# Routing's modality bias computed in the opening, its loads on another queue, and head 0's value rest released earlier

## The chip, the cores and the metric

The program runs on one core of a Trainium2 chip, in one launch. The metric is the device time of an execution in microseconds; of the kernel before there are three timed runs and one execution under the hardware profiler. The core's engines are TensorE (PE in the profile, PEld its weight loads), VectorE (DVE), ScalarE (ACT), GpSimd (POOL) and SyncE (SP), which here issues most DMAs. Each takes its own instructions in order.

## The reference, cut to what matters

Attention with rotary embedding over 2 batches x 8 heads of 576 tokens, then a mixture of 8 experts with one expert for each token, then a dense layer pair with a gate:

```
attn_out = softmax(rot(q) @ rot(k).T / 8) @ v          # 16 heads, 576 x 64 each
x = attn_out as (1152 tokens, 512)
logits = x @ w_gate + modality_bias[modality_id]       # 8 experts
e_idx = argmax(logits); gate_w = softmax(logits)[e_idx]
x = gate_w * (relu(x @ w1[e_idx]) @ w2[e_idx])
h = x @ w_in; g = h * tanh(softplus(h)); out = g @ w_out
```

The change touches how modality_bias[modality_id] comes to be: a table of 2 x 8 numbers, picked for each token by its modality of 0 or 1.

## The kernel before

**Arithmetic.** Products that need float32's accuracy are made of two halves: a rounded value ("hi") and the rest ("lo" = value - hi). So q, k, v, the exponentials and all weights are split by ScalarE, VectorE and GpSimd before TensorE takes them.

**Stages.** Attention's sixteen heads come first, up to about 165 us. The experts' tiles follow, then the gated layer pair. Routing of batch 0 is worked in between the later heads' work, as VectorE has room.

**Preparation of a head** n (heads 2 to 15): SyncE loads q and k as the tile xs (line 880) and v as vraw (line 884). GpSimd multiplies xs by the rotary tables (line 924), adds the halves (928), rounds (934) and takes the rest (943); both go into a tile ab, of which there is one. SyncE then copies ab into the "stack" that TensorE reads: the hi half of q (line 951, p_top), the lo half of q (959), and k hi and lo into sk twice (960, 961), all in p_stack. For v, GpSimd rounds (934, v_hi) and takes the rest (968, v_lo) into vhl. Two raw tiles vraw serve in turn: head 2's load needs head 0's tile, which its rounding and its rest read. Heads 0 and 1 are special: head 0 is rotated by p_first on VectorE, ScalarE and GpSimd without a stack; head 1 by VectorE and ScalarE, and its stack is copied as the others'.

**What follows in a head.** TensorE's scores (979) go to two PSUM tiles; VectorE takes the maximum (1003), ScalarE the exponential (1014); TensorE transposes (1027); ScalarE and VectorE split the transposed tile (1047, 1053); TensorE multiplies by v (1068), ScalarE evacuates (1077), TensorE transposes back with the gate's product appended (1098), VectorE normalizes into X (1108).

**What sets the order.** The class Plan does, when the program is built. Each step is an op with an engine, an assumed duration, a due key and the steps it depends on; the planner lets each engine take the step that could start first, or with the smaller key, and writes the instructions out in that order. Buffers and copies are steps or resources of it too (("vraw", n) is given back by the step vlo of the head two before). So an op's key, duration or dependency changes the order of all engines. What stands on an engine's list waits for semaphores at run time; a wait holds all that stands behind it there.

**The bias.** setup_ids issued two small loads from ScalarE's queue: the modalities (mod, 10 KB) and the two rows of the table spread to 128 partitions (mbias). setup_bias then worked on GpSimd: a cast, a comparison with 0 and one with 1, and for each batch two products and a sum, 40 elements wide. They stand in the plan as the ops ids (key 30) and bias (key 60, deps ids).

Of the kernel before, what the change touches and what calls it, by code (L numbers as in the profile page):

```python
# [10 lines left out]
F32 = mybir.dt.float32  # L11
# [3 lines left out]
ALU = mybir.AluOpType  # L15
# [3 lines left out]
B, H, S, D = 2, 8, 576, 64  # L19
HALF_D = D // 2  # L20
DM = H * D
NE = 8
# [190 lines left out]
def moe_kernel(ctx: ExitStack, tc: tile.TileContext, aps, out):  # L213
    nc = tc.nc
# [9 lines left out]
    kp = xctx.enter_context(tc.tile_pool(name="kp", bufs=1, side="right"))  # L224
# [16 lines left out]
    mod = kp.tile([128, B, 5, 2], I32, name="mod")  # L241
# [4 lines left out]
    def setup_consts():  # L246
        nc.vector.memset(zero, 0.0)
        nc.gpsimd.memset(ones, 1.0)
        nc.gpsimd.affine_select(
            out=upper, in_=ones, pattern=[[1, 128]], compare_op=ALU.is_gt, fill=0.0,  # L250
            base=0, channel_multiplier=-1,
        )
        nc.gpsimd.iota(
            iota8, pattern=[[0, 5], [1, NE]], base=-NE, channel_multiplier=0,
            allow_small_or_imprecise_dtypes=True,
        )
        nc.gpsimd.memset(iota8[64:128, 2, :], 1000.0)
        nc.gpsimd.iota(
            iotat, pattern=[[1, NS[1]]], base=0, channel_multiplier=0,
            allow_small_or_imprecise_dtypes=True,  # L260
        )
        for b in range(B):
            nc.gpsimd.memset(X[b][:, :, XC + 2:], 0.0)
            for j, (q0, _) in enumerate(QT):
                nc.gpsimd.iota(
                    X[b][:, j, XC:XC + 1], pattern=[[0, 1]], base=b * S + q0,
                    channel_multiplier=1, allow_small_or_imprecise_dtypes=True,
                )
    def setup_ids():
        nc.scalar.dma_start(  # L270
            out=mod.rearrange("p b j w -> p (b j w)"), in_=aps["modality"].bitcast(I32)
        )
        nc.scalar.dma_start(
            out=mbias.rearrange("p m e -> p (m e)"),
            in_=aps["modality_bias"].rearrange("(o m) e -> o (m e)", o=1).to_broadcast(
                [128, 2 * NE]
            ),
        )
# [8 lines left out]
        )  # L287

    def setup_bias():
        m = kp.tile([128, B, 5], F32, name="mf")  # L290
        sel = kp.tile([128, 2, B, 5], F32, name="msel")
        tmp = kp.tile([128, B, 5, NE], F32, name="mtmp")
        nc.gpsimd.tensor_copy(m, mod[:, :, :, 0])
        for v in range(2):
            nc.gpsimd.tensor_scalar(
                out=sel[:, v], in0=m, scalar1=float(v), scalar2=None, op0=ALU.is_equal
            )
        for b in range(B):
            sh = [128, 5, NE]
            for v, o in ((0, lbias), (1, tmp)):  # L300
                nc.gpsimd.tensor_tensor(
                    out=o[:, b], in0=sel[:, v, b, :, None].to_broadcast(sh),
                    in1=mbias[:, None, v].to_broadcast(sh), op=ALU.mult,
                )
            nc.gpsimd.tensor_tensor(out=lbias[:, b], in0=lbias[:, b], in1=tmp[:, b], op=ALU.add)


    regs = {}
# [518 lines left out]
    def attention(actx, hook):  # L827
# [26 lines left out]
        def setup_mov():  # L854
            for z in range(2):
                r = slice(z * 64, z * 64 + 64)
                nc.sync.dma_start(
                    out=mov[r, :, D:XW], in_=aps["w_gate"].rearrange("(h p) e -> p h e", p=D)
                )
                nc.vector.tensor_copy(  # L860
                    mov[r, :, 0:64],
                    ident[r, None, z * 64:z * 64 + 64].to_broadcast([64, H, 64]),
                )
# [252 lines left out]
        v_load(1)  # L1116
        p_load(2)
        setup_mov()
        setup_consts()
        p_first()  # L1120
        for n in range(2):
# [14 lines left out]
        def op(name, eng, dur, key, fn, *a, deps=(), line=None, **kw):  # L1136
            go = (lambda: fn(*a)) if isinstance(eng, str) else lambda: fn(*a, plan.eng)
            plan.op((name,) + a, eng, dur, key, go, deps=deps, line=line, **kw)

        for n in range(B * H):  # L1140
            z = 10.0 * n
            if n > 2:
                op("load", "sp", 0.45, z + K["ld"], p_load, n, take=[("xs", n)], tail=3.6, line="l")
            if n > 1:
                op("vload", "sp", 0.45, z + K["ld"], v_load, n, take=[("vraw", n)], tail=3.0, line="v",
                   deps=[("stack", 1)] * (n == 3))
            pr = K["prep"]
            if n > 1:
                op("mul", ("pool", "dve"), (2.67, 1.27), z + pr[0], p_mul, n,
                   deps=[("load", n)] + [("plo", 1)] * (n == 2))  # L1150
                op("add", ("pool", "dve"), (1.38, 0.67), z + pr[0], p_add, n, deps=[("mul", n)])
                op("phi", ("pool", "act"), (0.74, 0.573), z + pr[1], p_hi, n, deps=[("add", n)],
                   take=[("ab", n)])
                op("plo", ("pool", "dve"), (1.36, 0.669), z + pr[2], p_lo, n, deps=[("phi", n)],
                   give=[("xs", n)])
            if n == 1:
                plan.op(("add", 1), "dve", 0.67, -55.0, lambda: p_add(1, "dve"),
                        deps=[("mul", 1)])
                plan.op(("phi", 1), "act", 0.573, -50.0, lambda: p_hi(1, "act"),
                        deps=[("add", 1)], take=[("ab", 1)])  # L1160
                plan.op(("top", 1), "sp", 0.6, -50.0, lambda: p_top(1), deps=[("phi", 1)],
                        take=[("qs", 1)])
                plan.op(("plo", 1), "dve", 0.669, -50.0, lambda: p_lo(1, "dve"),
                        deps=[("phi", 1)], give=[("xs", 1)])
            if n:
                op("stack", "sp", 2.5, z + pr[3], p_stack, n, deps=[("plo", n)] + [("top", 1)] * (n == 1),
                   take=[("qs", n)] * (n > 1), give=[("ab", n)], tail=2.3)
            if n > 1:
                op("vhi", ("pool", "act"), (0.52, 0.36), z + pr[4], v_hi, n, deps=[("vload", n)],
                   take=[("vhl", n)])  # L1170
                op("vlo", ("pool", "dve"), (0.82, 0.402), z + pr[5], v_lo, n, deps=[("vhi", n)],
                   give=[("vraw", n)])
            else:
                op("vlo", "pool", 0.82, z + pr[5], v_lo, n, deps=[("vhi", n), ("plo", 1)],
                   give=[("vraw", n)])
        tiles, groups, was, e_was = 0, 0, (), ()
        for q in range(4 * (B * H) // 2):
# [53 lines left out]
            groups += len(u.groups)  # L1231
        for i in range(14):
            op("zero", "sp", 0.5, 20.0 + 5.0 * i, setup_dma, i, deps=[("stack", 3 + i // 3)])
        op("ids", "act", 0.1, 30.0, setup_ids)
        op("bias", "pool", 2.5, 60.0, setup_bias, deps=[("ids",)])
        hook(plan, bank, ltile)
        plan.run()

# [556 lines left out]
```

## Time and profile before

| | us |
|---|---|
| median of three runs (lowest, highest) | 485.17 (484.85, 485.33) |
| the profiled execution | 485.32 |
| its span, first to last instruction | 483.6 |
| TensorE busy | 464.2 (96%) |
| VectorE busy | 390.4 (81%) |
| GpSimd busy | 361.9 (75%) |
| ScalarE busy | 331.2 (68%) |

Busy shares are means over the whole span. TensorE's busy time is modelled and holds short gaps between matmuls, so what a stage is bound by is read from who waits for whom there. The chain of work that ended last is TensorE's for most of the second half of the program, with a part of VectorE's around 304 to 356 us; it can be followed back to 220 us, before which TensorE is busy nearly without a break to about 24 us.

### The profile page before, as it was taken

The numbers are of one execution on the slowest core, as the hardware profiler recorded it, in microseconds if no ns is written. First come the engines' busy times: TensorE is split into PE (matmuls) and PEld (weight loads), VectorE is DVE, ScalarE is ACT, GpSimd is POOL, SyncE is SP. The second block draws the span as 40 slices with busy tenths as digits, with TensorE's granted clock in tenths as the row PEclk, the third lists the DMA queues.
The fourth block names the chain that finished last, engine by engine and source line by source line (L and its number), as shares of the span: only waits on it lengthen the run. The fifth ranks groups of instructions, "written<-read, shape, count | busy, mean of one in ns | idle before, by whom it ended". The sixth has DMA issues, their size and how long they took to land.

```text
span 483.6 us, 8783 instructions
## 1 busy us (share of the span) xinstructions
PE 464.2 (96%) x2996; PEld 427.7 (88%) x2996; DVE 390.4 (81%) x616; ACT 331.2 (68%) x753; POOL 361.9 (75%) x363
## 2 busy tenths in 40 slices
PE   2799999999999999999999999999999999999995
PEld 1699999999998999999999998989889887888894
DVE  6599899798898765655888689999999859777773
ACT  3588888777878665475554587666675788776763
POOL 3799999999981588768767277786786749987654
PEclk9999999999999999999999999999999999999999
DMA  7689985877765399977974400202000001100002
GB/s 225 168 200 243 224 239 149 193 205 178 182 162 171 136 386 385 330 300 262 378 279 186 174 2 1 79 10 87 1 0 1 1 1 43 45 22 1 1 0 89
DMA packets 24131, 69.41 MB, mean 144 GB/s; under 512 B 5522, under 2 KB 9810, under 8 KB 22034
## 3 DMA queue, kind: packets, MB, share of 16 engines
q1 hardware_dynamic: 21794, 63.16, 42.1%
q0 software_dynamic: 1456, 5.03, 2.7%
q10 hardware_dynamic: 832, 0.61, 0.5%
q8 instruction: 25, 0.41, 0.3%
q14 instruction: 24, 0.20, 0.1%
HBM read 49.08 MB, written 6.44 MB: 115 GB/s over the span
## 4 chain that ended last, share of the span: by engine, by line
PE 41%; DVE 8%; issue 3%; POOL 1%; ACT 1%; POOLq 0%; DVEq 0%; ACTq 0%
PE h L1588 15%; PE o L1649 15%; PE mm L712 11%; DVE ta L1614 6%; DVE wc L1418 1%; DVE ta L1615 1%; POOL out_dram L1659 0%; DVE wc L1408 0%; PE mm L675 0%; DVE wc L1413 0%; POOLq L1791 0%; POOL g L1632 0%; DVE idi L1735 0%; ACT ot L1655 0%; DVE yl L1526 0%
## 5 line engine op out<-in xcount | busy, mean ns | idle before, releaser
L1614 DVE RECIPROCAL ta<-ta 128x320 f32<-128x320 f32 (+1 forms) x64 | 124.6, 1947 | 21.5 <-ACT ta L1607 20.0
L1562 POOL TENSOR_TENSOR w2l<-wc,w2h 128x512 fp32r<-128x512 f32 x64 | 89.3, 1417 | 15.3 <-ACT w2h L1561 15.3
L1649 PE MATMUL o<-w2h,g 128*128 128x512 f32 x288 | 97.8, 395 | 0.1
L1632 POOL TENSOR_TENSOR g<-ta,g 128x320 fp32r<-128x320 f32 (+1 forms) x63 | 52.7, 841 | 27.9 <-ACT g L1626 21.3
L979 PE MATMUL sc<-sk,sq 128*128 128x288 f32 (+1 forms) x320 | 59.4, 315 | 11.5 <-ACT sk L908 7.7
L1588 PE MATMUL h<-yl,w2h 128*128 128x320 f32 (+2 forms) x204 | 67.0, 328 | 0.1
L1588 PE MATMUL h<-yh,w2h 128*128 128x320 f32 (+2 forms) x204 | 66.9, 328 | 0.0
L1588 PE MATMUL h<-yh,w2l 128*128 128x320 f32 (+2 forms) x204 | 66.9, 328 | 0.0
L1649 PEld LDWEIGHTS o<-w2h,g 128*128 128x128 f32 x288 | 53.9, 188 | 12.2 <-POOL g L1632 1.0
L1047 ACT ACTIVATE ph<-pt 128x512 fp32r<-128x512 f32 (+2 forms) x112 | 54.8, 509 | 13.4 <-PE pt L1027 12.4
L1014 ACT ACTIVATE pexp<-sc,nm 128x576 f32<-128x576 f32 x72 | 53.3, 740 | 15.5 <-DVE nm L1003 11.7
L1003 DVE TENSOR_REDUCE nm<-sc 128x1 f32<-128x576 f32 x72 | 53.7, 753 | 10.8 <-PE sc L979 6.7
L979 PEld LDWEIGHTS sc<-sk,sq 128*128 128x128 f32 (+1 forms) x320 | 46.6, 190 | 14.3 <-ACT sk L908 8.1
L1649 PE MATMUL o<-w2l,g 128*128 128x512 f32 x144 | 56.8, 394 | 0.0
L1027 PE MATMUL pt<-ident,pexp 128*128 128x128 f32 (+1 forms) x360 | 55.0, 277 | 0.7 <-DVE tbl L523 0.6
L1068 PE MATMUL av<-ph,vhl 128*128 128x256 f32 (+1 forms) x160 | 50.7, 333 | 0.0
L1053 DVE TENSOR_TENSOR pl<-pt,ph 128x512 fp32r<-128x512 f32 (+1 forms) x80 | 48.8, 628 | 2.1 <-ACT ph L1047 1.8
L1027 PEld LDWEIGHTS pt<-ident,pexp 128*128 128x128 f32 (+1 forms) x360 | 42.1, 138 | 3.6 <-issue 0.7
L1626 ACT ACTIVATE g<-ta 128x320 fp32r<-128x320 f32 (+1 forms) x64 | 27.9, 436 | 22.9 <-DVE ta L1615 22.5
L1603 ACT ACTIVATE ta<-h 128x320 f32<-128x320 f32 (+1 forms) x64 | 25.5, 399 | 25.0 <-PE h L1588 23.5
L1588 PEld LDWEIGHTS h<-yl,w2h 128*128 128x128 f32 x204 | 38.3, 188 | 4.1 <-DVE yl L1526 0.4
L1588 PEld LDWEIGHTS h<-yh,w2h 128*128 128x128 f32 x204 | 38.3, 188 | 3.9 <-DVE ta L1615 0.2
(448 smaller groups left out, 1203.7 us busy)
## 6 DMA issues: line engine op xcount, KB each, us to landing
wr<-in_wio_dram SPq DMA_DIRECT2D x16, 1024.0 KB, 6.1
wc<-in_w_dram SPq DMA_DIRECT2D x26, 512.0 KB, 5.7
xs<-in_qk_dram SPq DMA_DIRECT2D x15, 576.0 KB, 5.2
sk<-ab SPq DMA_DIRECT2D x30, 288.0 KB, 3.3
sq<-ab SPq DMA_DIRECT2D x30, 144.0 KB, 2.4
vraw<-in_v_dram SPq DMA_DIRECT2D x16, 160.0 KB, 3.9
scratch<-zero SPq DMA_DIRECT2D x12, 108.8 KB, 4.8
xrow(0, 0)_2295<-scratch SPq DMA_DIRECT2D x2, 290.0 KB, 3.1
```

Of the source, the lines that this page charges most:

```text
L712: nc.tensor.matmul(ps[:, :T], lhsT=w, rhs=m, start=(n == 0), stop=(n == 3 * len(pairs) - 1))
L979: nc.tensor.matmul(t[:m, hf, :NC2], lhsT=sq[:, c:c + m], rhs=sk[:, z, hf * NC2:(hf + 1) * NC2], start=(z == 0), stop=(z == 1),)
L1003: nc.vector.tensor_reduce(out=nm[n, j], in_=sc[n, j][:, :, :NC2], axis=AX.XY, op=ALU.max, negate=True)
L1014: nc.scalar.activation(out=pe, in_=sc.pop((n, j))[:, :, :NC2], func=AF.Exp, bias=nm.pop((n, j)), accum_out=st[n, hf][:, i:i + 1],)
L1027: nc.tensor.transpose(out=t[:kn, o:o + 128], in_=pexp[n, j][:, k0:k0 + kn], identity=ident)
L1047: nc.scalar.activation(out=block(ph, n, hf, kts, slice(0, kn)), in_=psum(n, hf, kts, kn), func=AF.Copy)
L1068: nc.tensor.matmul(av[n, hf][:, :u.nq], lhsT=vhl[n][:, kt].rearrange("p a d -> p (a d)"), rhs=src[:, kt, u.at:u.at + u.nq], start=(kt == 0 ...
L1562: nc.gpsimd.tensor_tensor(out=lo[:, cs], in0=w[:, cs], in1=hi[:, cs].bitcast(F32), op=ALU.subtract)
L1588: nc.tensor.matmul(ps[:, :w], lhsT=wt[:, c], rhs=m[y][:, c], start=(n == 0), stop=(n == 11))
L1614: nc.vector.reciprocal(out=ta, in_=ta)
L1632: eng.tensor_tensor(out=gt[q][1][:, o:o + w], in0=tas.pop((q, i))[:, :w], in1=gt[q][0][:, o:o + w].bitcast(F32), op=ALU.subtract,)
L1649: nc.tensor.matmul(acc[g, t], lhsT=a[:, s], rhs=b, start=(f == 0 and z == 0), stop=(f == FC2 - 1 and z == 2),)
```

## The change

setup_ids moves from ScalarE's queue to SyncE's, behind the loads of the gate weights, and is called before the plan. setup_bias makes both products over both batches at once: six operations, the products and the sum 80 wide. Its op has the key -20, the duration 1.4 and no dependency. Head 0's value rest (vlo, 0) depends on head 1's addition instead of head 1's rest.

```diff
     def setup_ids():
-        nc.scalar.dma_start(
+        nc.sync.dma_start(
             out=mod.rearrange("p b j w -> p (b j w)"), in_=aps["modality"].bitcast(I32)
         )
-        nc.scalar.dma_start(
+        nc.sync.dma_start(
             out=mbias.rearrange("p m e -> p (m e)"),
...
     def setup_bias():
-        m = kp.tile([128, B, 5], F32, name="mf")
-        sel = kp.tile([128, 2, B, 5], F32, name="msel")
-        tmp = kp.tile([128, B, 5, NE], F32, name="mtmp")
-        nc.gpsimd.tensor_copy(m, mod[:, :, :, 0])
+        m = kp.tile([128, B * 5], F32, name="mf")
+        sel = kp.tile([128, 2, B * 5], F32, name="msel")
+        tmp = kp.tile([128, 2, B * 5, NE], F32, name="mtmp")
+        nc.gpsimd.tensor_copy(m, mod.rearrange("p b j w -> p (b j) w")[:, :, 0])
         for v in range(2):
             nc.gpsimd.tensor_scalar(
                 out=sel[:, v], in0=m, scalar1=float(v), scalar2=None, op0=ALU.is_equal
             )
-        for b in range(B):
-            sh = [128, 5, NE]
-            for v, o in ((0, lbias), (1, tmp)):
-                nc.gpsimd.tensor_tensor(
-                    out=o[:, b], in0=sel[:, v, b, :, None].to_broadcast(sh),
-                    in1=mbias[:, None, v].to_broadcast(sh), op=ALU.mult,
-                )
-            nc.gpsimd.tensor_tensor(out=lbias[:, b], in0=lbias[:, b], in1=tmp[:, b], op=ALU.add)
+        for v in range(2):
+            nc.gpsimd.tensor_tensor(
+                out=tmp[:, v], in0=sel[:, v, :, None].to_broadcast([128, B * 5, NE]),
+                in1=mbias[:, v, None].to_broadcast([128, B * 5, NE]), op=ALU.mult,
+            )
+        nc.gpsimd.tensor_tensor(
+            out=lbias.rearrange("p b j e -> p (b j) e"), in0=tmp[:, 0], in1=tmp[:, 1], op=ALU.add
+        )
...
         setup_mov()
+        setup_ids()
         setup_consts()
...
-                op("vlo", "pool", 0.82, z + pr[5], v_lo, n, deps=[("vhi", n), ("plo", 1)],
+                op("vlo", "pool", 0.82, z + pr[5], v_lo, n, deps=[("vhi", n), ("plo" if n else "add", 1)],
                    give=[("vraw", n)])
...
-        op("ids", "act", 0.1, 30.0, setup_ids)
-        op("bias", "pool", 2.5, 60.0, setup_bias, deps=[("ids",)])
+        op("bias", "pool", 1.4, -20, setup_bias, deps=[])
```

What this does to the order shows at three places. On SyncE's queue in the opening (mov are the gate weights, sq and sk the stack of head 1 as copied from ab, vraw a head's values, xs a head's q and k) there stood, before and now:

```order
L857 DMA mov<-in_w_gate_dram 64x8x8 x2
L951 DMA sq_201<-ab_192 64x576
L959 DMA sq_201<-ab_192 64x576
L960 DMA sk_202<-ab_192 64x1152
L961 DMA sk_202<-ab_192 64x1152
L884 DMA vraw_242<-in_v_dram 128x320
L880 DMA xs_250<-in_qk_dram 128x1152
```

```order
L857 DMA mov<-in_w_gate_dram 64x8x8 x2
L270 DMA mod<-in_modality_dram 128x20
L273 DMA mbias<-in_modality_bias_dram 128x16
L951 DMA sq_213<-ab_203 64x576
L884 DMA vraw_225<-in_v_dram 128x320
L959 DMA sq_213<-ab_203 64x576
L960 DMA sk_214<-ab_203 64x1152
L961 DMA sk_214<-ab_203 64x1152
L880 DMA xs_262<-in_qk_dram 128x1152
```

The two small loads come behind the gate weights, and head 2's value load has moved from behind head 1's stack to between its first copy and the other three.

On GpSimd in the opening, from the rest of head 0's q (sq) on (stt are sums of exponentials, rs their reciprocals to be, vhl the split values):

```order
L898 TENSOR_TENSOR sq_154<-xs_119,sq_154 64x320
L1086 TENSOR_SCALAR rs_1_211<-stt 128x2
L968 TENSOR_TENSOR vhl_172<-vraw_126,vhl_172 128x5x64
L924 TENSOR_TENSOR xs_130<-xs_130,tabs 128x1152
L928 TENSOR_TENSOR xs_130<-xs_130 128x576
L934 TENSOR_SCALAR ab_265<-xs_130 128x576
L943 TENSOR_TENSOR ab_265<-xs_130,ab_265 128x576
```

```order
L898 TENSOR_TENSOR sq_156<-xs_119,sq_156 64x320
L293 CAST mf<-mod 128x10
L295 TENSOR_SCALAR msel<-mf 128x10 x2
L299 TENSOR_TENSOR mtmp<-msel,mbias 128x80 x2
L303 TENSOR_TENSOR lbias<-mtmp 128x80
L968 TENSOR_TENSOR vhl_174<-vraw_126,vhl_174 128x5x64
L1086 TENSOR_SCALAR rs_1_223<-stt 128x2
L924 TENSOR_TENSOR xs_130<-xs_130,tabs 128x1152
```

The bias stands between the rest of q and head 0's value rest, and the value rest now comes ahead of the sums.

On TensorE, the first place where its order differs is between the scores of head 10 (counts are the routing's token counts, pt transposed exponentials):

```order
L979 MATMUL sc_111<-sk_1408,sq_1407 128x288 x4
L979 MATMUL sc_110<-sk_1408,sq_1407 128x288 x4
L1027 MATMUL pt_1_2_1628<-ident,pexp_3_1562 128x128
L1027 MATMUL pt_1_2_1628<-ident,pexp_4_1575 128x128
L1027 MATMUL pt_1_2_1628<-ident,pexp_3_1562 128x128
L1027 MATMUL pt_1_2_1628<-ident,pexp_4_1575 128x128
L1098 MATMUL xo_0_1633<-mov,avt_113 128x72 x3
```

```order
L979 MATMUL sc_111<-sk_1367,sq_1366 128x288 x4
L370 MATMUL counts<-oh_1582,ones 128x40
L371 MATMUL counts<-oh_1582,upper 128x40
L979 MATMUL sc_110<-sk_1367,sq_1366 128x288 x4
L1098 MATMUL xo_0_1651<-mov,avt_113 128x72 x3
```

The routing's counts come earlier, the transposes there later; from here on to the end of attention the order is another one, with the same work in it.

## Rows read from the trace of the kernel before

**Rows 1.** Busy time by stretch: start:end, length, engines' busy us (instructions), clock, DMA.

```profile
20.00:80.00 60.00, 58.81 (x473) 57.34 (x472) 51.75 (x104) 49.10 (x122) 56.17 (x67) 1.00 0.88 224
```

**Rows 2.** TensorE's waits, 7 to 190 us: total us, times, longest.

```profile
PE sc L979 <- DMA sk<-ab: 0.6, 1, 0.6
PE pt L1027 <- DVE tbl L523: 0.6, 1, 0.6
```

**Rows 3.** Line 961, the last copy of a stack: from issue to landing.

```profile
DMA to landing us min/median/max: 4.1/4.2/4.3
```

**Rows 4.** Timeline, SyncE's queue and TensorE around head 9: start, us, what, idle before.

```profile
85.33 0.60 SPq L961 DMA_DIRECT2D sk<-ab  x1
...
89.58 1.28 PE L979 MATMUL sc<-sk,sq 128*128 128x288 f32 x8 [0.61 <-DMA sk<-ab]
```

**Rows 5.** Timeline of TensorE in the opening.

```profile
14.17 1.06 PE L1027 MATMUL pt<-ident,pexp 128*128 128x128 f32 x4
...
19.76 0.67 PE L1098 MATMUL xo<-mov,avt 128*128 128x72 f32 x4 [0.47 <-ACT avt L1077]
20.22 1.82 PE L979 MATMUL sc<-sk,sq 128*128 128x288 f32 x12
23.23 0.79 PE L979 MATMUL sc<-sk,sq 128*128 128x288 f32 x4 [1.19 <-ACT pexp L1014]
23.86 1.15 PE L1027 MATMUL pt<-ident,pexp 128*128 128x128 f32 x9
```

**Rows 6.** Timeline of SyncE's queue in the opening.

```profile
4.59 1.32 SPq L857 DMA_DIRECT2D mov<-in_w_gate_dram  x2
...
14.33 0.50 SPq L959 DMA_DIRECT2D sq<-ab  x1
14.88 0.60 SPq L960 DMA_DIRECT2D sk<-ab  x1
15.54 0.59 SPq L961 DMA_DIRECT2D sk<-ab  x1
16.23 0.72 SPq L884 DMA_DIRECT2D vraw<-in_v_dram  x1
```

**Rows 7.** Timeline of GpSimd, the bias where it stood.

```profile
73.15 0.19 POOL L293 CAST mf<-mod 128x10 f32<-128x10 int32 x1
...
73.85 0.27 POOL L301 TENSOR_TENSOR lbias<-msel,mbias 128x40 f32<-128x40 f32 x1
74.06 0.27 POOL L301 TENSOR_TENSOR mtmp<-msel,mbias 128x40 f32<-128x40 f32 x1
74.41 0.27 POOL L305 TENSOR_TENSOR lbias<-lbias,mtmp 128x40 f32<-128x40 f32 x1
...
75.42 0.46 POOL L934 TENSOR_SCALAR vhl<-vraw 128x320 fp32r<-128x320 f32 x1
```

**Rows 8.** Timeline of GpSimd in the opening.

```profile
11.11 1.00 POOL L898 TENSOR_TENSOR sq<-xs,sq 64x320 fp32r<-64x320 f32 x1 [7.47 <-ACT sq L917]
14.43 0.22 POOL L1086 TENSOR_SCALAR rs<-stt 128x2 f32<-128x2 f32 x1 [2.31 <-ACT pexp L1014]
14.73 0.86 POOL L968 TENSOR_TENSOR vhl<-vraw,vhl 128x320 fp32r<-128x320 f32 x1
```

**Rows 9.** Line 968 (ns min/median/max); line 1562, 380 to 450 us; timeline at 308 us.

```profile
L968 POOL TENSOR_TENSOR vhl<-vraw,vhl x16: 858/874/884, 14.7 to 139.5; 128x320 fp32r<-128x320 f32 x16
...
L1562 POOL TENSOR_TENSOR w2l<-wc,w2h 128x512 fp32r<-128x512 f32 x24 | 30.6, 1295 | 2.8 <-ACT w2h L1561 2.8
...
308.08 3.53 POOL L1562 TENSOR_TENSOR w2l<-wc,w2h 128x512 fp32r<-128x512 f32 x2
...
308.50 1.97 DVE L1418 SCALAR_TENSOR_TENSOR wc<-wr,wc 128x1024 int32<-128x1024 int32 x1
```

**Rows 10.** Timeline of VectorE in the opening.

```profile
10.03 1.36 DVE L924 TENSOR_TENSOR xs<-xs,tabs 128x1152 f32<-128x1152 f32 x1
...
11.98 0.75 DVE L928 TENSOR_TENSOR xs<-xs 128x576 f32<-128x576 f32 x1
...
13.54 0.76 DVE L943 TENSOR_TENSOR ab<-xs,ab 128x576 fp32r<-128x576 f32 x1
```

## What was predicted

> **What bounds the kernel now.** I read the stretches first, then TensorE's waits, then the opening instruction by instruction. From 20 to 80 us TensorE is busy 58.81 of 60 us and GpSimd 56.17 of 60 [rows 1]: in attention both run almost without a break, and a reader could take either for the bound. TensorE's waits decide it [rows 2]: from 7 to 190 us it waits for the stacked copy of a head (the DMAs into sk) once only, for 0.6 us. All other heads are there when TensorE comes for them, so behind the opening TensorE sets the pace, and GpSimd keeps up closely without holding it. The one wait is head 9's: its last key copy is issued at 85.33 us and lands 4.2 us later, 89.53, and TensorE starts its scores at 89.58 after 0.61 us of idleness [rows 3, 4].
>
> The opening is different: there TensorE waits for a chain. It takes up head 1's first scores at 20.22 us, right behind the four products that end attention's first unit, and then stands still again until 23.23 for an exponential [rows 5]. Head 1's copies are issued at 14.33 (low half of q), 14.88 and 15.54 us (k twice) [rows 6], so the last one lands at 15.54 + 4.2 = 19.74. It is no more than 20.22 - 19.74 = 0.5 us early. **Whatever delays these three issues by more than 0.5 us moves everything behind it.** From 23.86 us TensorE has no long wait to swallow a shift, and the tail of the program hangs on TensorE's order, so such a shift goes to the end whole.
>
> **Part 1: the bias leaves the middle.** The old eight steps of setup_bias stand on GpSimd from 73.15 to 75.42 us, 2.27 us [rows 7], between two heads' preparation. Taking them out brings head 9's copies some 2.3 us forward, and so TensorE's wait of 0.6 us at 89.58 goes [rows 2, 4]. More can't come directly: no other wait on a stack is left. I book -0.6.
>
> **Part 2: the bias in the opening.** GpSimd's next work after the rest of head 0's q, which ends at 11.11 + 1.00 = 12.11, is at 14.43 us [rows 8]: a gap of 2.3 us. How long are the new operations? The cast and two compares are as before: 0.70 us from the cast's start to the first product's (73.15 to 73.85) [rows 7]. A 40-wide product follows the next after 0.21 us and takes 0.27; a 320-wide value rest takes 0.874 [rows 7, 9], which is (0.874 - 0.27) / 280 = 2.16 ns an element, so 80 wide is 0.09 us longer: 0.30 from one product to the next. The sum of two products starts 0.35 us after the second of them (74.06 to 74.41), 0.44 with the width, and leaves after 0.30. Together 0.70 + 0.30 + 0.44 + 0.30 = 1.74 us. Alone, they fit the gap: 12.11 + 1.74 = 13.85, and head 0's value rest, which before ran at 14.73, would run from 13.85 to 14.72. The two small loads are issued behind the gate weights (4.59 + 1.32 = 5.91 us) [rows 6], six us ahead of their use; I cost them at nothing. If they came late they would push the bias by as much.
>
> They are not alone. VectorE adds head 1's halves from 11.98 to 12.73 and takes its rest from 13.54 to 14.30 [rows 10], both with two inputs from SBUF, and the bias reads SBUF. What that does is seen later in this trace [rows 9]: a GpSimd rest w2l takes 1.295 us where VectorE decodes nothing, but a pair of them takes 3.53 us at 308.08, where VectorE starts a 1024-wide step with two SBUF inputs at 308.50. That step itself lasts 1.97 us. Read in turn: the first w2l to 309.38, then VectorE to 310.47 (1.09 us), then the second w2l. They alternate, one blocks the other. In the opening, too, q's rest of 320 elements takes 1.00 us beside the end of VectorE's long product [rows 8, 10], where a value rest of as many takes 0.874.
>
> [...]
>
> So the cast waits for 12.73 instead of 12.11 (0.62 us), and the second product waits while VectorE's rest, which comes at 13.54 during the first product (13.43 to 13.73), runs to some 14.45 (0.72 us). That is 1.34 us together: head 0's value rest runs from 15.19 to 16.06.
>
> **Part 3: what stands behind the value rest.** Head 0's rest no longer waits for head 1's rest in the plan but for its addition, so the planner thinks the buffer of raw values free earlier and puts head 2's value load between head 1's first q copy and its other three copies on SyncE's queue. That load must wait for head 0's value rest, which reads the buffer, and a waiting instruction holds all behind it. Before, the load came last, at 16.23 us, and held nothing [rows 6]. Now the low half of q is issued not at 14.33 but after the value rest (16.06 + 0.03), the load's own 0.72 us and 0.05 between issues: 16.86, 2.5 us later. The last key copy goes out at 18.07 and lands at 22.27, and head 1's scores start at 22.32 instead of 20.22: +2.1 us. Recorded ends reach 0.06 us past the next start (73.85 + 0.27 against 74.06) [rows 7], and two such seams lie in the sum, so I take **+2.0**. Bounds: without the exclusion the value rest ends at 14.72, the q copy goes at 15.52, 1.19 later, and the scores start at 20.98: +0.8. The load is of 160 KB and might slow the copies behind it; if it took its own issue time once more, +0.7 on top.
>
> GpSimd itself comes later with its next steps by as much, since its conversion of head 2 needs the buffer that head 1's copies read; head 2's and head 3's stacks then land about 2.1 to 2.5 us later, and TensorE comes 2.0 us later, so I expect at most some tenths of waiting there.
>
> **Part 4: the new order from about 100 us on.** The planner spreads the small change: TensorE's order is the same up to head 10's scores, then the routing counts come two groups of work earlier, and VectorE's table of tiles comes earlier too. Work is equal. What an order can shed or add is waits like the one on the table (0.6 us) [rows 2]; I take 0, with 0.9 us either way.
>
> **Sum.** The profiled execution took 485.32 us with a span of 483.6; the median of three is 485.17, 0.15 below. 485.32 + 2.0 - 0.6 = 486.7, less 0.15: **486.6 us**, slower by 0.3%.
>
> **Rivals.**
> *No exclusion in the opening.* The bias instructions are short and may slip between VectorE's reads; then 485.17 + 0.8 - 0.6 = 485.4, no change. For it: the rows that show blocking are of long operations; against it: q's rest of 1.00 us in the same stretch. Chance 0.25.
> *GpSimd is the bound after all.* Then its 2.27 us come off, and the new order also loses its waits: 485.17 - 2.27 = 482.9. This is the faster side. It decides if heads in general, not one, are waited for. For it: 56.17 of 60 us busy [rows 1]; against: one wait of 0.6 us for sixteen heads [rows 2], and the later copies of head 1 hit GpSimd first. Between 482.9 and 484.3 lies also a new order that sheds the waits of rows 2 while the opening costs only 0.8. Chance 0.13.
> *The clock falls.* TensorE now idles some 2 us before 22.3, on top of the 1.19 us before the next scores. [...] Chance 0.05.
> *The new order is worse* by over a us: 487.8. Chance 0.05. The forecast keeps 0.52.
>
> **How the numbers follow.** A measurement of this kernel can tell 0.2%, 0.97 us. The forecast with its scatter of 0.9 lies above 486.14 two times in three (0.34); with the clock, the worse order and a few hundredths of the first rival, slower is 0.48. Within 0.2%: the rest of the forecast (0.17), most of the first rival (0.18), some of the second: 0.38. Faster: 0.14. The range that leaves out the second rival's lower part and the clock is 484.3 to 487.8; its lower part is the first rival less 0.9 and its upper one the forecast plus 0.9 and some of the load's 0.7.
>
> **What would show it.** In the profile after: the value load ahead of head 1's other copies on SyncE's queue, issued when head 0's value rest ends (16.1; at 14.7 there was no exclusion); VectorE's rest of head 1 longer than 0.76 us, or gaps between the bias operations; TensorE's first scores of head 1 at 22.3 us (21.0 by the first rival); no wait at head 9. Wrong it is if the scores start by 20.5, or if heads 2 to 8 begin to wait for stacks by more than some tenths, or if the shift of the opening is gone by 160 us.

## The result, and the profile of the changed kernel

The changed kernel takes 490.89 us (median of four runs, 489.23 to 492.72) where the kernel before, timed beside it, takes 485.25 (484.85 to 485.37): ratio 1.0118, interval 1.0103 to 1.0133. It is slower by 5.6 us; forecast were 486.6 and a range of 484.3 to 487.8. The four runs also spread over 3.5 us, and with them goes TensorE's mean granted clock: 489.23 (0.999), 490.06 (0.999), 491.72 (0.996), 492.72 (0.992). The profiled execution is the fastest of them, with a span of 487.5 us, 3.9 more than before; it shows the part of the loss that the clock has nothing to do with. One slow run of all that were timed, 763.92 us at a clock of 0.564 in the kernel of "The bias planned", is left out of the ratios and ranges below.

TensorE's waits from 7 to 190 us in the changed kernel (total us, times, longest), which answer [rows 2]:

```profile
PE pt L1027 <- DVE pl L1053: 1.7, 5, 0.5
PE sc L979 <- DMA sk<-ab: 1.2, 1, 1.2
PE sc L1319 <- DVE xg(0, 0)_2365 L1308: 1.1, 1, 1.1
```

The two waits of before (0.6 for head 9's stack, 0.6 for the routing's table) are gone. In their place stand one for head 1's stack, five for VectorE's rest of the transposed exponentials (pl), and one for xg, the expert's input that VectorE scales by the gate.

The opening of the changed kernel, against [rows 5, 6, 8, 10]; first VectorE, then GpSimd, SyncE's queue and TensorE:

```profile
11.84 0.75 DVE L928 TENSOR_TENSOR xs<-xs 128x576 f32<-128x576 f32 x1
...
13.40 0.76 DVE L943 TENSOR_TENSOR ab<-xs,ab 128x576 fp32r<-128x576 f32 x1
```

```profile
12.04 0.60 POOL L293 CAST mf<-mod 128x10 f32<-128x10 int32 x1
12.73 0.48 POOL L295 TENSOR_SCALAR msel<-mf 128x10 f32<-128x10 f32 x2
13.18 1.16 POOL L299 TENSOR_TENSOR mtmp<-msel,mbias 128x80 f32<-128x80 f32 x2
14.42 0.35 POOL L303 TENSOR_TENSOR lbias<-mtmp 128x80 f32<-128x80 f32 x1
14.73 0.86 POOL L968 TENSOR_TENSOR vhl<-vraw,vhl 128x320 fp32r<-128x320 f32 x1
```

```profile
13.39 0.53 SPq L951 DMA_DIRECT2D sq<-ab  x1
15.62 0.33 SPq L884 DMA_DIRECT2D vraw<-in_v_dram  x1
16.04 0.51 SPq L959 DMA_DIRECT2D sq<-ab  x1
...
17.23 0.59 SPq L961 DMA_DIRECT2D sk<-ab  x1
```

```profile
21.38 1.85 PE L979 MATMUL sc<-sk,sq 128*128 128x288 f32 x12 [1.25 <-DMA sk<-ab]
```

The cast takes 0.60 us instead of 0.19 and ends right behind VectorE's addition (11.84 + 0.75 = 12.59). The two products take 1.16 us and end at 14.34, right behind VectorE's rest (13.40 + 0.76 = 14.16), which itself takes no longer than before. The value load stands in front of the stack's other copies and goes out when head 0's value rest ends (15.59); the stack lands 4.1 to 4.2 us [rows 3] after 17.23, at 21.3 to 21.4, and TensorE starts at 21.38 where it started at 20.22.

How far the changed kernel is behind at later places (starts in the changed kernel less those before): head 1's first scores 21.38 - 20.22 = 1.16; head 9's 90.22 - 89.58 = 0.64, since the wait in front of them is gone; the first expert's first product, the row below, 167.52 - 163.17 = 4.35; the end 3.9. So some 3.7 us are lost between 90 and 168 us, where the prediction had put nothing. The first product of line 712, before and changed:

```profile
163.17 0.39 PE L712 MATMUL mm<-xh(0, 0)_2502,whi(0, 0)_0_2371 128*128 128x304 f32 x1
```

```profile
167.52 0.38 PE L712 MATMUL mm<-xh(0, 0)_2501,whi(0, 0)_0_2313 128*128 128x304 f32 x1
```

### The profile page after: what moved, and what is told of

It is laid out like the page before. It is cut to its first block, busy times and chain, and to the rows that moved or that the text cites. A ratio compares the mean times of both kernels' runs of the same rounds, so it can differ in the third digit from the quotient of the medians.

```text
span 487.5 us, 8780 instructions
## 1 busy us (share of the span) xinstructions
PE 465.1 (95%) x2996; PEld 428.0 (88%) x2996; DVE 391.9 (80%) x616; ACT 332.4 (68%) x753; POOL 361.8 (74%) x360
## 4 chain that ended last, share of the span: by engine, by line
PE 52%; POOL 0%; issue 0%; ACT 0%; POOLq 0%; DVE 0%
PE h L1588 21%; PE o L1649 20%; PE mm L712 11%; POOL out_dram L1659 0%; PE mm L675 0%; POOLq L1791 0%; ACT ot L1655 0%; DVE yl L1526 0%; ACT yh L1524 0%; ACT Y L762 0%; POOL spacer L1666 0%; POOLq L1659 0%
## 5 line engine op out<-in xcount | busy, mean ns | idle before, releaser
L1614 DVE RECIPROCAL ta<-ta 128x320 f32<-128x320 f32 (+1 forms) x64 | 124.6, 1947 | 22.3 <-ACT ta L1607 22.3
L1562 POOL TENSOR_TENSOR w2l<-wc,w2h 128x512 fp32r<-128x512 f32 x64 | 90.3, 1431 | 16.4 <-ACT w2h L1561 16.4
L1632 POOL TENSOR_TENSOR g<-ta,g 128x320 fp32r<-128x320 f32 (+1 forms) x63 | 51.7, 825 | 27.7 <-ACT g L1626 21.1
L1588 PEld LDWEIGHTS h<-yh,w2l 128*128 128x128 f32 x204 | 38.4, 188 | 2.3
```

Of the source, the lines that this page charges most:

```text
L1562: nc.gpsimd.tensor_tensor(out=lo[:, cs], in0=w[:, cs], in1=hi[:, cs].bitcast(F32), op=ALU.subtract)
L1588: nc.tensor.matmul(ps[:, :w], lhsT=wt[:, c], rhs=m[y][:, c], start=(n == 0), stop=(n == 11))
L1614: nc.vector.reciprocal(out=ta, in_=ta)
L1632: eng.tensor_tensor(out=gt[q][1][:, o:o + w], in0=tas.pop((q, i))[:, :w], in1=gt[q][0][:, o:o + w].bitcast(F32), op=ALU.subtract,)
```

## Experiments

Each was timed beside the kernel before on the same chip. Since that kernel's median moved a little between the three groups (484.98, 485.22, 485.18), differences to it are what is compared across groups.

### The bias alone, in the old order

```diff
+        setup_ids()            # behind setup_mov(), on SyncE
...
         p_mul(1, "dve")
+        setup_bias()           # the six operations
...
-        op("ids", "act", 0.1, 30.0, setup_ids)
-        op("bias", "pool", 2.5, 60.0, setup_bias, deps=[("ids",)])
+        op("ids", "act", 0.1, 30.0, lambda: None)
+        op("bias", "pool", 2.5, 60.0, lambda: None, deps=[("ids",)])
```

> The order of the kernel before on every engine, word for word, but the bias as six GpSimd operations behind the rest of head 0's q, its two loads on SyncE behind the gate weights, and nothing of it in the middle; the value rest and head 2's load stay where they were. Theory (the loss is made by the load in front of head 1's stack and by the new order from 90 us on, not by the bias): head 1's scores start at 20.2 us as before, GpSimd is some 0.3 us later at 16 us and 2 us earlier behind 76 us, the 0.6 us of waiting for head 9 goes, 484.6 us. Rival (the bias itself hurts in the opening, through the exclusion with VectorE): the scores of head 1 or of head 2 start more than 0.5 us later than before (20.22 and 28.15), 485.3 us or more.

Measured: 484.46 us (11 runs, 484.14 to 485.19), ratio 0.9991 (0.9982 to 1.0000), 0.52 less than before. Head 1's scores start at 19.93, right behind the products ahead of them; at 89 us the scores of head 9 follow without a wait. The bias itself is a small gain, just what part 1 of the prediction booked (0.6), although its operations are stretched by VectorE here as above (cast 0.60, products 1.16).

### The opening alone

```diff
         def p_top(n):
             ...
+            if n == 1:
+                v_lo(0)
+                v_load(2)
```

with the planner's own steps for both left empty, on top of the bias alone.

> As e1_bias_alone, and head 0's value rest ahead of the sums with head 2's value load between the first and the second copy of head 1's stack, as in the changed kernel; the order behind 20 us stays that of the kernel before. Theory (two losses that add: opening +1.2, later order some +3): head 1's scores at 21.4 us, a shift of 1.2 us that stays to the end, 1.2 over e1_bias_alone, 485.8 us. Rival (the stalls from 95 us on follow from the late opening, not from the order): stalls of TensorE on VectorE's pl appear here too and the time is 488 us or more.

Measured: six runs, each with its granted clock: 485.43 (1.000), 486.46 (0.994), 486.86 (0.994), 487.40 (0.991), 488.15 (0.990), 488.66 (0.988); median 487.13, ratio 1.0052 (1.0038 to 1.0066). The profiled run is the first. TensorE's waits in it hold the stack's 1.2 us and nothing of the new ones behind it:

```profile
PE sc L982 <- DMA sk<-ab: 1.2, 1, 1.2
...
PE pt L1030 <- DVE tbl L523: 0.6, 1, 0.6
```

So the opening costs 485.43 - 484.46 = 1.0 us where the clock holds (the spans of the two profiled executions differ by as much, 483.7 - 482.7), and the late stalls don't follow from it. The time falls as the clock rises, run by run.

### The load behind the stack

```diff
             nc.sync.dma_start(out=sk[64:128].bitcast(F32), in_=a[64:128])
+            if n == 1:
+                v_load(2)
```

with the planner's step for it left empty, in the changed kernel.

> The changed kernel with one instruction moved: head 2's value load is issued behind the four copies of head 1's stack instead of behind the first. All else stands in the changed kernel's order. Theory (opening and order add): head 1's scores at 20.2 us, 1.2 us less than the changed kernel, 488.0 us at its best, with the stalls behind 95 us still there. Rival (the late stalls are a consequence of the opening): 485 us. If the scatter of the changed kernel's runs (489.2 to 492.7, granted clock 0.999 to 0.992) comes of TensorE's idle time in the opening, the runs here agree within 0.3 us with a clock of 0.998 or more; if it comes of a later stall, they scatter as much as before.

Measured: 489.57 us (489.32 to 490.64, four runs, clocks 0.996 to 0.999), ratio 1.0102 (1.0087 to 1.0116), 4.59 over before. Head 1's scores start at 20.29 again, but the time is not 1.2 us below the changed kernel's profiled run: the gain of the opening is given back at once. Three of the four runs lie within 0.42 us; the slowest, 490.64, has the clock of 0.996, so some of the scatter does not hang on the wait at 20 us. No profile shows where that run lost its clock. GpSimd and SyncE's queue of this kernel around 20 us, and TensorE's first scores of head 2, here, in the kernel of "The rest held" and before:

```profile
20.34 0.46 POOL L934 TENSOR_SCALAR vhl<-vraw 128x320 fp32r<-128x320 f32 x1
20.77 0.87 POOL L970 TENSOR_TENSOR vhl<-vraw,vhl 128x320 fp32r<-128x320 f32 x1
21.61 0.66 POOL L934 TENSOR_SCALAR ab<-xs 128x576 fp32r<-128x576 f32 x1
```

```profile
21.66 0.33 SPq L884 DMA_DIRECT2D vraw<-in_v_dram  x1
...
24.95 0.59 SPq L961 DMA_DIRECT2D sk<-ab  x1
```

```profile
29.19 0.77 PE L981 MATMUL sc<-sk,sq 128*128 128x288 f32 x4 [0.72 <-ACT ph L1049]
```

```profile
28.80 0.77 PE L991 MATMUL sc<-sk,sq 128*128 128x288 f32 x4 [0.54 <-DMA sk<-ab]
```

```profile
28.15 0.78 PE L979 MATMUL sc<-sk,sq 128*128 128x288 f32 x4
```

The planner had also put two steps on values (0.46 + 0.87 us) ahead of head 2's rounding (the 0.66 us at 21.61), and they come ahead of head 2's copies. Its last key copy lands at 24.95 + 4.2 = 29.15 and TensorE starts at 29.19; the row names ScalarE's ph, but in the kernel of "The rest held" below, with the same opening, the wait there, 0.54 us, is put down to the DMA into sk. From head 1's first scores to head 2's it is 8.90 us here and 28.15 - 20.22 = 7.93 in the kernel before. In the changed kernel the two delays lie on top of each other (29.34 - 21.38 = 7.96 from head 1's scores to head 2's): the price of the opening is about one us either way. To get it back in this order, the values would have to go behind head 2's rounding as well; no run tried both.

### The changed kernel again

> The changed kernel once more, to see how far its runs scatter and where. Theory: between 489 and 493 us, each run's time going with its granted clock (0.007 of clock to 3 us); if the execution profiled here is one of the slower ones, the stretch where TensorE's granted clock is at the lower level shows which idle time came before it. Rival: the scatter was the chip's, and all runs lie near 489.3 us.

Measured: six runs, 488.59 to 494.24, median 490.64, ratio 1.0124 (1.0095 to 1.0154); clocks 0.999 to 0.985. The slowest runs have the lowest clocks (491.63 at 0.990, 494.24 at 0.985), but 490.00 has 0.999 and 490.65 has 0.996. The profiled execution, 490.64 us, has a clock of 0.989. Its stretches from 18 to 32 us (busy time and count of PE, PEld, DVE, ACT, POOL; granted clock; DMA share; GB/s):

```profile
18.00:20.00 2.00, 1.53 (x9) 1.12 (x8) 0.45 (x2) 0.67 (x3) 1.92 (x3) 1.00 1.03 210
20.00:22.00 2.00, 0.83 (x4) 0.76 (x4) 0.31 (x1) 0.00 (x0) 1.79 (x3) 0.64 0.94 288
22.00:24.00 2.00, 2.00 (x10) 1.95 (x9) 0.45 (x1) 0.00 (x0) 1.92 (x3) 0.50 0.75 213
24.00:30.00 6.00, 5.25 (x23) 4.87 (x23) 3.91 (x7) 3.85 (x9) 4.00 (x4) 0.50 0.86 220
30.00:32.00 2.00, 2.00 (x15) 1.83 (x14) 1.16 (x3) 1.35 (x3) 1.76 (x4) 0.80 0.02 5
```

```profile
21.22 3.25 PE L979 MATMUL sc<-sk,sq 128*128 128x288 f32 x12 [1.17 <-DMA sk<-ab]
...
32.55 0.78 PE L979 MATMUL sc<-sk,sq 128*128 128x288 f32 x4
```

Two finer stretches show when it falls:

```profile
20.00:20.50 0.50, 0.06 (x1) 0.00 (x0) 0.31 (x1) 0.00 (x0) 0.50 (x2) 1.00 0.95 184
20.60:21.20 0.60, 0.00 (x0) 0.00 (x0) 0.00 (x0) 0.00 (x0) 0.59 (x1) 0.50 0.88 261
```

The granted clock falls from 1.00 to 0.50 while TensorE waits for head 1's stack, 0.5 us into that wait, and stays there to some 31 us. The twelve score products take 3.25 us instead of 1.85, and head 2's first scores start at 32.55 instead of 29.34: 3.2 us. In the other profile of the same kernel it stays at 1.00 through a wait of 1.25 us and on to 32 us, so what is measured here is that it can fall, not that it must.

Of the 3.2 us only 1.4 are left at the first expert's first product (168.93 against 167.52) and at the end (spans of 488.9 and 487.5). TensorE's wait of 1.1 us for xg is missing in this execution (see "The rest held"): the losses do not simply add.

### The idle time filled

In the order of the opening alone, ten transposes of the identity, whose results are overwritten.

```diff
             sc[n, j] = ltile[j] = t = scp[spare[2] % 2]
+            if n == 1 and not filled:                  # first try
+            if (n, j) == (0, QMIX):                    # second try, instead
+                for _ in range(10):
+                    nc.tensor.transpose(out=t[:, 0, 0:128], in_=ident, identity=ident)
```

> The kernel e2_opening_alone with ten transposes of the identity on TensorE in front of head 1's first scores, into the bank that these scores overwrite, so that the 1.2 us in which TensorE waits for the stack are mostly filled with work that nothing uses. Theory (the scatter of the changed kernel and of e2_opening_alone, 485.4 to 488.7, is TensorE's clock, which falls in some runs after that idle time, as the profile of e4_changed_again shows it at 21 to 30 us with a granted clock of 0.50): with the idle time filled every run keeps a clock of 0.997 or more and takes 485.3 to 486.0 us, though the scores start at 21.4 as before. Rival (the clock falls for another reason): 485.4 to 488.7 with clocks down to 0.988 again.

Measured: 487.75 us (486.59 to 488.33, clocks 0.995 to 0.999). This tells nothing on the clock's cause: the scores that wait for head 1's stack belong to a tile that it shares with head 0, so the transposes stood behind the wait, and the 1.34 us in front of it stayed. The second try puts them into it:

> e5_idle_filled put its ten transposes behind the wait instead of into it. Here they stand where TensorE waits: in front of the first eight score products that read head 1's stack (from 20 us on), in e2_opening_alone's order otherwise. Theory (the clock falls in some runs after TensorE's idle time of 1.2 us in the opening): the wait for the stack shrinks below 0.5 us, head 1's scores start at 21.4 as in e2_opening_alone, and all runs take 485.3 to 486.0 us with a clock of 0.997 or more. Rival (the clock falls for another reason): 485.4 to 488.7 with clocks down to 0.988.

```profile
20.14 1.25 PE L995 MATMUL sc<-ident 128*128 128x128 f32 x10
21.37 1.85 PE L982 MATMUL sc<-sk,sq 128*128 128x288 f32 x12
```

Measured: 486.33 us (11 runs, 485.71 to 487.08), ratio 1.0026 (1.0017 to 1.0035), all clocks from 0.997 to 1.000. The scores start no earlier than in the opening alone, yet the runs at 0.988 to 0.994 are gone, and with them 1.0 us of excess over the kernel before (1.15 instead of 2.15). This idle time is what lets the clock fall in the opening; the next one, 1.18 us in front of the scores at 24.40, is still there, and the clock holds. The median is 0.3 over the upper end of what was expected: with the clock held, the opening costs 1.15 + 0.52 = 1.7 here against 1.0 in the fastest run of the opening alone. Why it is 0.7 more is not shown.

### The rest held

In the kernel with the load behind the stack, GpSimd's rest wlo of the first weight chunk waits until VectorE's third gating step is done.

```diff
-        eng.tensor_tensor(out=lo, in0=w, in1=hi.bitcast(F32), op=ALU.subtract)
+        if (k, i) == ((0, 0), 0): pend.append(rest)    # rest: the line above
+        else: rest()
...
+            if i == 1:                                 # the third gating step
+                nc.gpsimd.tensor_copy(hold, xg[0][0:1, 1, 0:1])
+                pend.pop()()
```

> The kernel e3_load_behind, with GpSimd's rest of the first expert's first weight chunk (wlo) held until VectorE's third gating step xg is done (a copy of one element that reads xg stands in front of it). Theory (GpSimd's wlo and VectorE's xg exclude each other, and TensorE's wait of 1.1 us at 159 us is VectorE's xg waiting through wlo: 2.01 us instead of 0.47): every xg takes 0.47 us, TensorE's wait there goes, and 1.0 to 1.3 us come off 489.57: 488.4 us. Rival (wlo is what the experts' first products wait for, so holding it costs as much at 167 us): 489.3 us or more.

The steps xg of VectorE and wlo of GpSimd, first the two fences of the changed kernel, then the two of this one:

```profile
156.84 2.01 DVE L1308 TENSOR_SCALAR xg(0, 0)_2365<-xrow(0, 0)_2239 128x512 f32<-128x512 f32 x1
```

```profile
156.19 2.37 POOL L613 TENSOR_TENSOR wlo(0, 0)_0_2397<-wraw(0, 0)_0_2301,whi(0, 0)_0_2313 128x1024 fp32r<-128x1024 f32 x1 [1.61 <-issue]
```

```profile
156.78 0.47 DVE L1320 TENSOR_SCALAR xg(0, 0)_2366<-xrow(0, 0)_2240 128x512 f32<-128x512 f32 x1
158.55 0.46 DVE L1320 TENSOR_SCALAR xg(0, 0)_2366<-xrow(0, 0)_2240 128x512 f32<-128x512 f32 x1
```

```profile
159.22 2.37 POOL L617 TENSOR_TENSOR wlo(0, 0)_0_2398<-wraw(0, 0)_0_2302,whi(0, 0)_0_2314 128x1024 fp32r<-128x1024 f32 x1
```

Measured: 487.80 us (487.01 to 487.94), 2.58 over before instead of 4.59: 2.0 us less, more than the 1.0 to 1.3 expected (the two profiled executions have spans of 487.6 and 486.2, 1.4 less). VectorE's step is back at 0.47 us and TensorE's wait for it is gone. In the changed kernel VectorE's step, which reads one tensor from SBUF, began 0.65 us into GpSimd's and ended 0.29 us behind its end: 2.01 us for a step of 0.47.

Why the two meet: ScalarE rounds the chunk (whi, which wlo needs) at 157.42 us in the kernel before and at 155.00 in the changed one. Before, wlo began at 158.55, behind the third gating step (157.59).

```profile
157.42 1.05 ACT L608 ACTIVATE whi(0, 0)_0_2371<-wraw(0, 0)_0_2358 128x1024 fp32r<-128x1024 f32 x1
```

```profile
155.00 1.05 ACT L608 ACTIVATE whi(0, 0)_0_2313<-wraw(0, 0)_0_2301 128x1024 fp32r<-128x1024 f32 x1
```

Which of the two comes first also changes from one execution to another. In the second profile of the changed kernel, with TensorE late from the opening on, whi comes at 158.21 and wlo starts 0.12 us after this step of VectorE instead of 0.65 us ahead of it. The step takes 0.47 us, and now wlo is the longer one, 2.58 us instead of 2.37:

```profile
159.28 0.47 DVE L1308 TENSOR_SCALAR xg(0, 0)_2365<-xrow(0, 0)_2239 128x512 f32<-128x512 f32 x1
```

```profile
159.40 2.58 POOL L613 TENSOR_TENSOR wlo(0, 0)_0_2397<-wraw(0, 0)_0_2301,whi(0, 0)_0_2313 128x1024 fp32r<-128x1024 f32 x1 [1.98 <-ACT whi(0, 0)_0_2313 L608]
```

### The dependency alone, and with the rest held

```diff
-                   deps=[("vhi", n), ("plo", 1)],
+                   deps=[("vhi", n), ("plo" if n else "add", 1)],
```

in the kernel before, the planner free to order the rest.

> The kernel before with the dependency of head 0's value rest alone changed (head 1's addition instead of its rest) and the planner free to make its order; the bias stays in the middle. Theory (the opening's loss needs both parts, since without the bias GpSimd is at the value rest by 12.1 us and head 2's load is issued at 13.1, before the second copy of the stack): head 1's scores at 20.2 us, a steady clock; the later order is a new one again and may cost up to 4 us, 485 to 489 us. Rival (the dependency alone puts the stack late): scores at 21 us or later, clocks that scatter.

Measured: 487.87 us (485.97 to 490.34, clocks 1.000 to 0.989), ratio 1.0043 (1.0024 to 1.0062). No wait for head 1's stack: without the bias the value rest ends at 13.2 us and the load goes out at 13.93, with the next copy at 14.55. Yet the clocks scatter. The profiled run is the one of 490.34; its gating step, TensorE behind it, and the stretches (columns as above):

```profile
157.24 2.52 DVE L1308 TENSOR_SCALAR xg(0, 0)_2437<-xrow(0, 0)_2314 128x512 f32<-128x512 f32 x1
```

```profile
159.81 1.38 PE L1319 MATMUL sc<-ident,xg(0, 0)_2437 128*128 128x128 f32 x5 [1.54 <-DVE xg(0, 0)_2437 L1308]
```

```profile
158.00:160.00 2.00, 0.46 (x4) 0.15 (x2) 2.00 (x3) 0.70 (x2) 1.47 (x1) 1.00 0.00 0
160.00:162.00 2.00, 2.00 (x10) 1.46 (x9) 0.84 (x3) 0.78 (x3) 0.00 (x0) 0.58 0.77 248
162.00:170.00 8.00, 8.00 (x34) 7.27 (x34) 3.86 (x12) 3.18 (x6) 4.40 (x2) 0.50 0.43 148
170.00:172.00 2.00, 2.00 (x14) 2.00 (x13) 0.85 (x3) 0.42 (x1) 0.33 (x1) 0.86 0.88 324
```

The same collision again, in another order, and behind it ten us at a clock of 0.50. The clock falls at 160.3 us, when TensorE has been at work again for 0.5 us. With wlo held as above:

> e7_dependency_alone (486.0 to 490.3, clocks of 0.989 to 1.000) with GpSimd's rest of the first weight chunk held until VectorE's third gating step is done, as in e6_rest_held. Theory (in that order the only thing that is worse than before is the collision at 157 us: 1.5 us of idle TensorE, and in some runs the clock at 0.50 from 161 to 170 us behind it): the wait of 1.5 us goes, the clock stays at 0.997 or more in all runs, and as TensorE is 0.7 us ahead of the kernel before at 155 us, the time is 484.0 to 484.6 us. Rival (the scatter of clocks comes from the opening): clocks of 0.99 again and 485 to 489 us.

Measured: 484.56 us (11 runs, 483.62 to 484.81), ratio 0.9984 (0.9975 to 0.9993), all clocks 0.997 to 1.000. One wait in the right place turns a loss of 2.65 us into a gain of 0.62. The fastest run without it, 485.97 at a clock of 1.000, is 0.75 over before, so some 1.4 us of the 3.3 are the wait itself and the rest is the clock behind it. This version beats the kernel before and the changed one.

### The bias planned, without the dependency

The changed kernel with the value rest's dependency put back to `("plo", 1)`.

> The changed kernel with the dependency of head 0's value rest put back, the planner free: the bias in the opening, head 1's stack and head 2's load in the old order, and a new order from about 70 us on. Theory (a new order costs as such, because VectorE's and GpSimd's steps fall on each other anew): 20.2 us for head 1's scores and 2 us or more over e1_bias_alone (484.46), which has the same work in the old order. Rival (the changed kernel's order was an unlucky one): within 1 us of 484.5.

Measured: ratio 1.0083 (1.0065 to 1.0102), some 4 us over before, runs from 488.53 to 491.10. The opening is the old one, and the same bias in the old order gained 0.5: this loss of 4.5 us is made by the order and by what the clock does in it. The collision is there a third time (TensorE waits 1.55 us for xg), and the granted clock is 0.50 from 161.0 to 164.4 us.

### The sums first

In the kernel with the rest held, the sums of exponentials that VectorE's reciprocal needs at 113 us go ahead of head 13's addition on GpSimd.

```diff
         def p_add(n, eng="pool"):
+            if n == 13 and not late:
+                late.append(lambda: p_add(n, eng))     # issued behind the next sums
+                return
```

> e6_rest_held with two GpSimd steps of the changed order swapped: the sums (rs) that VectorE waits for at 113 us go ahead of head 13's addition (1.41 us) instead of behind it. Theory (VectorE stands 0.8 us for these sums there, and TensorE then waits twice for VectorE's pl, 0.24 and 0.53 us): both waits shrink or go, 0.5 to 1.0 us less than 487.8. Rival (the waits on pl come of VectorE's own order): 487.8.

Measured: 488.73 us (488.61 to 489.22), 3.55 over before instead of 2.58: worse by 1.0. The theory fell. What the sums are made of isn't ready earlier: GpSimd now stands still 0.97 us for it, the sums come only 0.4 us earlier (112.76 against 113.16) and the addition 1.4 us later (113.07 against 111.67):

```profile
112.76 0.23 POOL L1103 TENSOR_SCALAR rs<-stt 128x3 f32<-128x3 f32 x1 [0.97 <-ACT pexp L1031]
113.07 1.43 POOL L943 TENSOR_TENSOR xs<-xs 128x576 f32<-128x576 f32 x1
```

What else the late order loses, some 2 us (4.1 by the sum below, less the collision's 2.0), stays open. TensorE's waits on pl (1.7 us in five in the changed kernel, 1.4 in four with the rest held) are the largest that are left; which of VectorE's steps should stand elsewhere was not found.

## Why the prediction was wrong

**The sum as measured.** Differences to the kernel before, each from runs beside it: the bias out of the middle -0.5 (the bias alone); the opening with the clock held +1.0 (the opening alone, fastest run); the order behind 90 us +4.1 (load behind the stack less bias alone, 4.59 + 0.52 = 5.1, less the 1.0 that head 2's stack costs in it); the clock that falls in the opening +1.0 in the median (changed kernel 5.64 less load behind the stack 4.59). Forecast were -0.6, +2.0, 0 and nothing. The terms add up to the 5.64 measured because the last two are taken as differences, so their sum proves nothing. Two other readings bear the sizes out: in the changed kernel's profile, where the clock holds, 3.7 us are lost between 90 and 168 us; and of the ten runs of the changed kernel, the four with a clock of 0.998 or more are 3.6 to 5.0 over before (median 4.4), all ten 5.7 in the median, which leaves 1.3 to the clock.

**What bounds the kernel, and part 1: right.** TensorE sets the pace, head 9's wait went, and no more came of GpSimd's 2.27 us. The rival that GpSimd is the bound is out: the bias alone gains 0.5.

**Part 2, the exclusion (GpSimd and VectorE by turns, as read from [rows 9]): right in kind.** Cast and second product wait for VectorE's addition and rest. VectorE's rest did not wait in its turn, as the prediction had it: it took 0.76 us as before. The value rest came at 14.73, forecast at 15.19 - 0.14 = 15.05 in this trace's time (q's rest starts 0.14 earlier than in rows 8): the blocked product had already started, and the sum follows 0.08 us behind its end. The loads cost nothing, but by little: in the kernel with the load behind the stack the cast waits for the modalities until 12.75 and then takes 0.19 us; as q's rest starts 0.26 us later there (11.23 against 10.97), that is the same end as here behind VectorE's addition (12.94 - 0.26 = 12.68 against 12.64).

**Part 3: right mechanism, half the size, and half of the story.** The load took 0.33 us of the queue instead of 0.72, and with the earlier value rest the low half of q went out at 16.04 instead of 16.72: +1.2 us at the scores, not +2.1. The start of the scores, 21.38, is nearer to the 21.0 of the rival without exclusion than to 22.3; that there was one is seen from the cast and the second product, not from this time. What was missed: the same edit puts two value steps ahead of head 2's rounding on GpSimd. "At most some tenths" was said of head 2; it is 1.0 us once head 1 is on time, hidden in the changed kernel because head 1 is late as well.

**The rival of the clock: right in kind, the chance wrong.** It was given 0.05. That idle time can bring the clock down no row of the kernel before shows: the 1.19 us in [rows 5] left it at 1.00. The second profile of the changed kernel shows it, with 0.50 in a wait of 1.17 us, and the spacing of the transposes bears the column out: nine of them span 2.12 us at 26.35, where it has 0.50, against 1.15 us in [rows 5], where it has 1.00. (Four span 1.06 us at 14.17 in [rows 5], although the column has 1.00 there too; why is not shown.) With a second wait of 1.2 us in front of the one of 1.19, by the mean clocks it fell in all but one of the six runs of the opening alone, and they are 1.0 to 3.2 us longer. In the changed kernel's median it makes 1.0 to 1.3 us.

**Part 4: the step that failed.** "Work is equal. I take 0, with 0.9 us either way", and a chance of 0.05 for 487.8. The 0 was mis-sized: the order cost some 4 us (4.1 by the medians, 3.7 in the profile). Equal work on each engine is not equal time where one engine's step holds up another's, as here (2.01 us for 0.47): 1.4 to 2.0 us of it come of GpSimd's wlo on VectorE's xg, as holding wlo shows, and the rest stays open. A warning was in [rows 9], where two GpSimd rests of 1.295 us take 3.53 beside a VectorE step; the prediction used it in the opening alone, where it could see the pair, and did not ask what new pairs the order makes. That a VectorE step with one input is held as well, [rows 9] do not show. Three of three new orders by the planner (changed kernel, dependency alone, bias planned) made the same pair at 157 us in a profiled execution, and in two of them the profile shows the clock falling behind it.

## What to carry to other kernels

When a planner reorders a tuned kernel, look through the new order for pairs such as those met here: a long GpSimd step beside a VectorE step that reads two tensors from SBUF ([rows 9]: two rests of 1.295 us took 3.53), or scales one there as xg does (2.01 us for 0.47). Where TensorE waits for the shorter step, the rest of the longer one is an estimate of the price: in the changed kernel 1.7 of wlo's 2.37 us were left when xg began, xg took 1.5 us longer, and TensorE waited 1.1 us for it. Holding one of the two for the other can be worth more than the edit itself: here it turned a loss of 2.65 us into a gain of 0.62. A new TensorE wait such as those of 1.2 to 1.6 us here has two prices, the wait and, in some runs, the granted clock behind it (0.50 for 3.4 to ten us in three profiled executions), so read the clock of every timed run and not of the profiled one alone.

## What the runs showed of the hardware that was not expected

TensorE's granted clock can fall to 0.50 in or behind an idle time of 1.2 to 1.6 us, in some executions of a program and not in others. In the first profile of the changed kernel it stayed at 1.00 through a wait of 1.25 us at 20 us. It fell 0.5 us into a wait of 1.17 us at 20 us in the second, then ten us at 0.50; 0.5 us after the end of a wait of 1.54 us at 158 us with the dependency alone, then again ten us; and 0.9 us after the end of one of 1.55 us with the bias planned, then 3.4 us. Ten transposes that nobody reads, put into the first idle time, kept all of eleven runs at 0.997 or more. And a VectorE step with one input from SBUF, begun while a GpSimd step of 2.4 us ran, took 2.01 and 2.52 us instead of 0.47.
